# A list scheduler's model of a shared port, and new due steps, in a fused attention and gated-MLP kernel

## The chip, the cores and the metric

The kernel runs on one core of one Trainium2 chip. The metric is the device time of one execution in microseconds (us); the median of three executions is given. PE is the matmul engine (TensorE), DVE VectorE, ACT ScalarE, POOL GpSimd, SP SyncE, whose queue issues nearly all DMAs here. PSUM is the memory that matmuls write, SBUF the one that they read.

## The reference

Cut to what is computed:

```python
B, H, S, Ns, D = (8, 8, 512, 32, 64)          # x: B H S D, state: B H Ns D
scores = scale * np.matmul(x, state.transpose(0, 1, 3, 2))
a = softmax(scores)                            # over Ns
xread = np.matmul(a, state)
scores2 = scale * np.matmul(state, x.transpose(0, 1, 3, 2))
a2 = softmax(scores2)                          # over S
sread = np.matmul(a2, x)
attn = np.concatenate([xread, sread], axis=2)
x2 = attn.transpose(0, 2, 1, 3).reshape(B * (S + Ns), H * D)    # 4352 x 512
h = x2 @ w_in                                  # w_in: 512 x 2048
g = h * np.cos(h)
return (g @ w_out).astype(np.float32)          # w_out: 2048 x 512
```

`x` and `state` are float32; `w_in` and `w_out` come as float64, so the kernel turns their bits into float32 itself.

## The kernel before

For each of the eight batches the kernel does the attention, then makes `h` in tiles of 128 of the 2048 columns by the 512 tokens: 16 tiles a batch. `products` multiplies the states into `w_in`, so that a tile needs only the attention weights `aT` and those products `sw` (L488). Batches go in pairs. For the first pair a tile is 512 columns wide and has one of two PSUM banks; later tiles are done two at a time and partly with seven instead of eight block products (`seven_part`, L543). Each tile then goes through four gate steps: ACT makes a whole number of turns of `h` (`gate`, L564), DVE takes the difference (`gate2`, L567), ACT takes a sine (`gate3`, L570), DVE multiplies with `h` into `g_all` (`gate4`, L584). `gate4` is the last reader of the bank, so tile n + 2 can start on PE when `gate4` of tile n is done. Tiles are numbered from 0; the first pair has 32.

The second product, `g @ w_out`, has two forms. The first pair's batch 0 multiplies directly (`first_product` and `second_product`, L640). All others use sums of blocks (`Product`), whose matmuls are L772 and whose sums of `g_all` are L715 (POOL, some DVE). The block sums of `w_out` are made by `inner_weight` (L689) and `sums_of` (L1325), sent to DRAM (L677, L692) and fetched back into a ring (L706).

Eighteen conversions turn float64 pieces of `w_in` and `w_out` into float32. Each is a DMA of the raw bits (`fetch`, L210), two ACT steps (L223, L226), two DVE steps ("b" L229, "c" L232) and a POOL step ("d", L237). Raw pieces share buffers, so a later fetch waits for the L232 of the piece before it in the buffer.

The order of the first pair's work is not written out by hand. `first_pair_tasks` lists tasks with an engine, an assumed cost, what they read and write, and a due step; `link` derives the dependencies and turns due steps into due times; `first_pair` then goes through model time and picks for each engine the task that comes next, and issues it. A task with `shares` set is one of DVE that uses the SBUF port that DVE and POOL share. `CONV` and `CONV_DUE` give the order of the conversions and their due steps, `PACE` the model time of one step, `NEAR` how far apart starts may lie to be chosen between. The engines run what they get in order; the waits on the chip follow from the data alone, and the model's times are nowhere in the program. From step 32 on, `later_pair` and fixed plans (`plan`, `plan_products`) set the order.

The choice in the model, word for word:

```python
                soon = min(starts.values())
                t = min((t for t in mine if starts[t] <= soon + NEAR),
                        key=lambda t: t.due + 1.0 * (starts[t] - soon))
                if best is None or starts[t] < best[0]:
                    best = starts[t], t
```

The softmax of a batch's first scores goes through `shift` (L348), `exp1` (L352), `sums1` (L325), an inverse (L373, L374), `spread1` (L332) and `norm1` (L393); that of the second through `max2` (L343), `exp2` (L361), `turn` (L400), `turn_kept` (L405), `reads` (L417), `keep_scaled` (L436). `tokens` (L271) and `tokens_kept` (L280) turn a batch's tokens, which L1180 loads.

Of the kernel before, what the change touches and what calls it, by code (L numbers as in the profile page):

```python
# [22 lines left out]
def kernel(  # L23
# [46 lines left out]
    TEMPS = 4  # L70
# [5 lines left out]
    def matrix(n):  # L76
        return quad(n).rearrange("p t (u d) -> p (t u) d", d=HD)
# [972 lines left out]
    for n in range(B // 2):  # L1050
        end = n == B // 2 - 1
# [71 lines left out]
    def first_pair_tasks():  # L1123
# [49 lines left out]
        def attention(b, k):  # L1173
# [26 lines left out]
            for j in range(2 if b == 0 else 0):  # L1200
                add("act", act(512) + .03,
                    lambda j=j: a.exp1(slice(j, j + 1)), f"z{z}{j}",
                    f"z{z}{j}", k + 4)
            m2 = k + 6 if b == 0 else k + 5
            if b == 0:
                for j in range(2):
                    add("dve", .62, lambda j=j: a.sums1((j,)), f"z{z}{j}",
                        f"m1{j}", k + 5)
                add("dve", .46, a.inverse1, "m10 m11", "m10 m11", k + 5)
                for j in range(2):  # L1210
                    add("dve", .62, lambda j=j: a.spread1(slice(j, j + 1)),
                        f"m1{j}", f"xT{j}", k + 5)
                for j in range(2):
                    add("dve", .62, lambda j=j: a.norm1(slice(j, j + 1)),
                        f"z{z}{j} xT{j}", f"z{z}{j}", k + 5, True)
# [3 lines left out]
            if b == 0:  # L1219
                add("act", .2, a.exp2_bias, "m20 m21", "m20 m21", m2)  # L1220
                for j in range(2):
                    add("act", .72, lambda j=j: a.exp2((j,)),
                        f"at{j} m2{j}", f"xT{2 + j} i2{j} T", m2)
                add("dve", .3, a.inverse2, "i20 i21", "i20 i21", m2 + 2)
            else:
                add("act", 5.0, a.exps, "at0 at1 m20 m21",
                    f"z{z}0 z{z}1 xT2 xT3 i20 i21 m20 m21", m2)
                for j in range(2):
                    add("dve", .62, lambda j=j: a.sums1((j,)), f"z{z}{j}",
                        f"m1{j}", k + 6)  # L1230
                add("dve", .8, a.inverse12, "m10 m11 i20 i21",
                    "m10 m11 i20 i21", k + 7)
                for j in range(2):
# [215 lines left out]
        for step, what in (  # L1449
# [6 lines left out]
                                "sd00 sd01", "stT1", 6)),  # L1456
                (5, lambda: attention(1, 5.0)),
                (7, lambda: products(0, 2, 7)),
# [6 lines left out]
                (16, lambda: products(1, 1, 19)),  # L1465
                (16, lambda: inner(3, matrix(SQ), SQ, temps[1], E, 15)),
                (17, lambda: sums_of(A22, SQ, A11, sub_, 18, "pool")),
                (17, lambda: attention(2, 18)),
                (18, lambda: sums_of(A21, A11, A21, sub_, 19, "dve")),
                (20, lambda: products(1, 2, 23)),  # L1470
                (20, lambda: inner(5, matrix(A21), A21, temps[0],
                                   names(TEMPS), 20)),
                (20, lambda: sends(1, a12, 6, 22)),
# [4 lines left out]
                (24, lambda: products(1, 3, 27)),  # L1478
                (25, lambda: attention_late(2, 23.0)),
                (24, lambda: [add("sp", .4, lambda n=n: fetch_block(n), "B3",  # L1480
# [3 lines left out]
        for step, what in (  # L1484
                (26, lambda: outer(0, 2, 0, 0, 26, "dve")),
                (27, lambda: outer(0, 2, 0, 1, 27, "dve")),
                (28, lambda: tokens_of_next(30)),
                (28, lambda: products(2, 0, 28)),
                (28, lambda: p5_tasks(29.5)),
                (29, lambda: weight_columns(t32, 30)),  # L1490
                (29, lambda: add("dve", .7, lambda: halves(2, 0), "z00 z01",
                                 "E0", 30)),
                (29, lambda: add("dve", .7, lambda: halves(2, 1),
                                 "z00 z01 E0", "E1", 30)),
                (30, lambda: seven_tasks(t32, 30)),
                (31, lambda: weight_columns(t34, 32)),
                (32, lambda: outer(2, 3, 2, 0, 32, "dve")),
                (32, lambda: p3_sums(32))):
            at_step[step].append(what)
        for step, t in enumerate(all_tiles[0:FIRST]):  # L1500
            for what in at_step[step]:
                what()
            tile_(t, step)
            if 4 <= step < 4 + NH:
                first(step - 4, step + 1)
            for i in range(NH):
                if SECOND_AT[i] == step:
                    second(i, step + 2)
        for what in at_step[FIRST]:
# [4 lines left out]
    CONV = (4, 5, 6, 7, 8, 9, 10, 11, 14, 15, 16, 17, 12, 13)  # L1514
    CONV_DUE = (3, 4.5, 3.5, 6, 7.5, 7, 9, 9.5, 10.5, 11, 12, 14.5, 14, 15)
    PACE, NEAR, SEND = 3.8, 0.3, 2.5

# [36 lines left out]
    def first_pair():  # L1554
# [19 lines left out]
        lanes = 22.0  # L1574
        pool_busy, cold = (0.0, 0.0), True
        log = []
        while can:
            best = None
            for e in free:
# [4 lines left out]
                for t in mine:  # L1584
                    at_ = max(free[e], ready[t])
                    if t.shares and pool_busy[0] <= at_ < pool_busy[1]:
                        at_ = pool_busy[1]
                    starts[t] = at_
                soon = min(starts.values())
                t = min((t for t in mine if starts[t] <= soon + NEAR),  # L1590
                        key=lambda t: t.due + 1.0 * (starts[t] - soon))
                if best is None or starts[t] < best[0]:
# [13 lines left out]
            if t.engine == "pool":  # L1606
                pool_busy = at_, end
            if t.engine == "sp":
                size = {"x": .13, "Q": 1.05, "B": .26, "r": .26}.get(
# [137 lines left out]
```

## Time and profile before

| what | before |
|---|---|
| median of 3 executions | 740.53 us |
| lowest and highest | 739.6 and 740.9 us |
| profiled execution, its own time | 740.65 us |
| its span, from first to last instruction | 738.9 us |
| mean granted clock of PE | 0.993 |
| PE waiting for L584 in 20 to 165 us | 12.3 us, 9 times |
| L584 of tiles 2, 9, 16, 24, 31 ends at | 40.6, 73.8, 105.4, 140.4, 163.6 us |

The durations that follow come from the one profiled execution. Times inside it count from its first instruction. A busy PE in the profile is not a PE at its peak, since matmuls overlap; what counts for PE is its idle time and its clock.

### The profile page before, as it was taken

To read this page: it belongs to the slowest core of one execution; us is meant where nothing else is said; L and a number is where in the kernel's file an instruction comes from. 1 tells how busy PE (TensorE), PEld (TensorE's weight loads), DVE (VectorE), ACT (ScalarE), POOL (GpSimd) and SP (SyncE) were. 2 spreads that over 40 slices of the span, in tenths; PEclk is the share of its full clock that TensorE was granted. 3 is DMA by queue.
4 is the path that set the end of the run, shared out by engine and by line. 5 is a ranking of instruction groups with operands and counts; after the bars stand their busy time and mean duration, and the time that the engine had idled before them with its cause. 6 is when DMAs were issued, how large, how long until landed. Compare 5 with 4: busy or idle time off the path is not lost.

```text
span 738.9 us, 10734 instructions
## 1 busy us (share of the span) xinstructions
PE 708.2 (96%) x3626; PEld 519.0 (70%) x3626; DVE 506.8 (69%) x703; ACT 347.3 (47%) x586; POOL 542.5 (73%) x524
## 2 busy tenths in 40 slices
PE   8898889999999999999999999999999999999997
PEld 3343343477778878777778788777688788888886
DVE  4989979957866668849756577768665467355550
ACT  5799675654463446343634464344634533211110
POOL 1557789375998997588998665879989665799600
PEclk9999999999999999999999999999999999999999
DMA  9966799536346964693238635762225466456662
GB/s 297 285 192 193 236 265 301 122 96 150 87 128 117 214 172 115 142 197 86 82 80 168 160 96 116 147 154 83 75 68 119 115 205 143 108 156 203 155 152 46
DMA packets 204021, 111.33 MB, mean 151 GB/s; under 512 B 149888, under 2 KB 166784, under 8 KB 203968
## 3 DMA queue, kind: packets, MB, share of 16 engines
q1 hardware_dynamic: 202880, 110.14, 57.4%
q8 instruction: 29, 0.48, 0.3%
q10 hardware_dynamic: 960, 0.39, 0.2%
q14 instruction: 24, 0.20, 0.1%
q0 software_dynamic: 128, 0.13, 0.1%
HBM read 87.03 MB, written 23.59 MB: 150 GB/s over the span
## 4 chain that ended last, share of the span: by engine, by line
PE 59%; POOL 21%; DVE 9%; issue 3%; DMA 3%; ACT 2%; SPq 1%; ACTq 0%; POOLq 0%; DVEq 0%
PE o L772 29%; POOL g_all L715 16%; PE h L543 13%; PE h L488 8%; POOL swS_all L521 3%; PE at L312 3%; PE at L877 2%; DMA held<-in_state_dram 2%; PE o L640 2%; POOL sw_all L521 2%; DVE g_all L715 1%; PE at L417 1%; DVE q_all L567 1%; DVE g_all L232 1%; DVE g_all L584 1%
## 5 line engine op out<-in xcount | busy, mean ns | idle before, releaser
L715 POOL TENSOR_TENSOR g_all<-g_all 128x512 f32<-128x512 f32 x252 | 332.5, 1349 | 61.8 <-DVE g_all L715 40.4
L772 PE MATMUL o<-g_all 128*128 128x256 f32 x1456 | 343.7, 381 | 2.4 <-POOL g_all L715 2.4
L772 PEld LDWEIGHTS o<-g_all 128*128 128x128 f32 x1456 | 273.7, 190 | 49.7 <-issue 5.7
L567 DVE TENSOR_TENSOR q_all<-q_all,h 128x1024 f32<-128x1024 int32 (+1 forms) x88 | 85.3, 971 | 40.7 <-ACT q_all L564 40.4
L564 ACT ACTIVATE q_all<-h 128x1024 int32<-128x1024 f32 (+1 forms) x88 | 73.1, 833 | 81.2 <-PE h L543 35.1
L584 DVE TENSOR_TENSOR g_all<-h,q_all 128x1024 f32<-128x1024 f32 (+1 forms) x88 | 85.7, 973 | 24.5 <-ACT q_all L570 23.6
L570 ACT ACTIVATE q_all<-q_all,halfpi 128x1024 f32<-128x1024 f32 (+1 forms) x88 | 84.2, 957 | 38.7 <-DVE q_all L567 38.5
L551 DVE TENSOR_TENSOR h<-h,sums_all 128x256 f32<-128x256 f32 x96 | 41.3, 430 | 77.5 <-PE h L543 60.2
L488 PE MATMUL h<-aT_all,sw_all 128*128 128x512 f32 x128 | 64.0, 628 | 13.0 <-DVE g_all L584 12.3
L543 PE MATMUL h<-aT_all,sw_all 128*128 128x256 f32 x192 | 59.6, 392 | 3.8 <-DVE g_all L584 3.4
L543 PE MATMUL h<-aS_all,swS_all 128*128 128x256 f32 x192 | 60.2, 395 | 2.6 <-ACT sums_all L529 1.8
L715 DVE TENSOR_TENSOR g_all<-g_all 128x1024 f32<-128x1024 f32 x42 | 62.0, 1490 | 0.1
L543 PE MATMUL h<-aS_all,sw_all 128*128 128x256 f32 x192 | 58.0, 384 | 0.1
L488 PEld LDWEIGHTS h<-aT_all,sw_all 128*128 128x128 f32 x128 | 23.2, 195 | 44.3 <-issue 21.5
L521 POOL TENSOR_TENSOR swS_all<-sw_all 128x128 f32<-128x128 f32 x48 | 22.5, 468 | 41.8 <-ACT sw_all L462 41.8
L543 PEld LDWEIGHTS h<-aS_all,swS_all 128*128 128x128 f32 x192 | 33.9, 189 | 27.0 <-issue 12.1
L780 ACT COPY o<-o 128x256 f32<-128x256 f32 x26 | 9.3, 357 | 85.1 <-PE o L772 85.1
L543 PEld LDWEIGHTS h<-aT_all,sw_all 128*128 128x128 f32 x192 | 34.5, 189 | 16.3 <-DVE g_all L584 12.2
L237 POOL TENSOR_TENSOR w_in<-w_in,aS_all 128x1024 int32<-128x1024 int32 (+1 forms) x10 | 22.3, 2241 | 29.9 <-DVE w_in L232 27.2
L787 ACT COPY o<-sums_all 128x256 f32<-128x256 f32 x26 | 9.8, 378 | 68.2 <-PE o L772 68.2
L543 PEld LDWEIGHTS h<-aS_all,sw_all 128*128 128x128 f32 x192 | 35.6, 190 | 8.2 <-DVE h L551 2.7
L607 DVE SCALAR_TENSOR_TENSOR held<-o,held 128x512 f32<-128x512 f32 x38 | 25.9, 681 | 13.7 <-PE o L772 13.1
(116 smaller groups left out, 931.6 us busy)
## 6 DMA issues: line engine op xcount, KB each, us to landing
g_all<-blocks_kept SPq DMA_DIRECT2D x206, 256.0 KB, 2.8
blocks_kept<-g_all SPq DMA_DIRECT2D x48, 256.0 KB, 3.9
g_all<-in_moe_w_out_dram SPq DMA_DIRECT2D x8, 1024.0 KB, 5.7
out_dram<-ot SPq DMA_DIRECT2D x128, 64.0 KB, 2.0
g_all<-in_moe_w_in_dram SPq DMA_DIRECT2D x6, 1024.0 KB, 7.1
x_b<-in_x_dram SPq DMA_DIRECT2D x24, 256.0 KB, 4.7
xT<-in_x_dram SPq DMA_DIRECT2D x80, 64.0 KB, 2.8
x_b<-in_x_dram SPq DMA_DIRECT2D x16, 128.0 KB, 4.3
```

The lines of the kernel that those rows point to most:

```text
L237: nc.gpsimd.tensor_tensor(bits, bits, e, op=ALU.add)
L488: nc.tensor.matmul(out=t.hp, lhsT=t.lhs(i), rhs=t.rhs(i), start=(i == 0), stop=(i == t.kn - 1))
L521: nc.gpsimd.tensor_tensor(o, x1, x2, op=op)
L543: nc.tensor.matmul(out=out_, lhsT=w, rhs=r, start=start, stop=True, skip_group_check=True)
L551: nc.vector.tensor_tensor(o, h2[:, LO], sums_all[:, 0], op=ALU.add)
L564: nc.scalar.activation(t.q.bitcast(I32), t.hp, func=ACTF.Copy, bias=0.25)
L567: nc.vector.tensor_tensor(t.q, t.q.bitcast(I32), t.hp, op=ALU.subtract)
L570: nc.scalar.activation(t.q, t.q, func=ACTF.Sin, bias=halfpi, scale=-TWO_PI)
L584: nc.vector.tensor_tensor(g, t.hp, t.q, op=ALU.mult)
L607: nc.vector.scalar_tensor_tensor(out=out.t[:, ch], in0=bank, scalar=TWO_PI, in1=b.t[:, ch], op0=ALU.mult, op1=ALU.add)
L715: engine.tensor_tensor(o[:, i:i + n], x1[:, i:i + n], x2[:, i:i + n], op=ALU.subtract)
L772: nc.tensor.matmul(out=o, lhsT=ring[(self.first + k) % NB][:, i], rhs=g[:, i], start=(start and i == 0), stop=(i == QT - 1), skip_group_ch ...
```

## The change

Only the planner of the first pair is edited. In its model, a POOL task now waits while a DVE task that shares the port runs, as DVE's sharing tasks already did for POOL's; among tasks that can start nearly together, a later start weighs 8.0 instead of 1.0 against the due time. The small inverses and the halves are marked as sharing. Due steps of conversions, of two attention parts, of weight sums, of the direct products and of product p5 are set anew, and `PACE` goes from 3.8 to 4.0. The tasks themselves, what they compute and their assumed costs stay. Line numbers after the edit are those of before up to L1203; `sums_of` goes from L1325 to L1327.

```diff
-            m2 = k + 6 if b == 0 else k + 5
+            m2 = k + 6 if b == 0 else k + 4
...
-                add("dve", .46, a.inverse1, "m10 m11", "m10 m11", k + 5)
+                add("dve", .46, a.inverse1, "m10 m11", "m10 m11", k + 5,
+                    True)
...
-                add("dve", .3, a.inverse2, "i20 i21", "i20 i21", m2 + 2)
+                add("dve", .3, a.inverse2, "i20 i21", "i20 i21", m2 + 2,
+                    True)
...
                 add("dve", .8, a.inverse12, "m10 m11 i20 i21",
-                    "m10 m11 i20 i21", k + 7)
+                    "m10 m11 i20 i21", k + 7, True)
...
-                (5, lambda: attention(1, 5.0)),
+                (5, lambda: attention(1, 4)),
...
-                (16, lambda: inner(3, matrix(SQ), SQ, temps[1], E, 15)),
+                (16, lambda: inner(3, matrix(SQ), SQ, temps[1], E, 18.5)),
                 (17, lambda: sums_of(A22, SQ, A11, sub_, 18, "pool")),
-                (17, lambda: attention(2, 18)),
+                (17, lambda: attention(2, 19)),
...
                 (20, lambda: inner(5, matrix(A21), A21, temps[0],
-                                   names(TEMPS), 20)),
+                                   names(TEMPS), 20.5)),
...
-                (25, lambda: attention_late(2, 23.0)),
+                (25, lambda: attention_late(2, 27)),
...
-                (28, lambda: p5_tasks(29.5)),
+                (28, lambda: p5_tasks(30.5)),
...
                 (29, lambda: add("dve", .7, lambda: halves(2, 0), "z00 z01",
-                                 "E0", 30)),
+                                 "E0", 30, True)),
                 (29, lambda: add("dve", .7, lambda: halves(2, 1),
-                                 "z00 z01 E0", "E1", 30)),
+                                 "z00 z01 E0", "E1", 30, True)),
...
             if 4 <= step < 4 + NH:
-                first(step - 4, step + 1)
+                first(step - 4, step + 3)
             for i in range(NH):
                 if SECOND_AT[i] == step:
-                    second(i, step + 2)
+                    second(i, step + 2.5)
...
     CONV = (4, 5, 6, 7, 8, 9, 10, 11, 14, 15, 16, 17, 12, 13)
-    CONV_DUE = (3, 4.5, 3.5, 6, 7.5, 7, 9, 9.5, 10.5, 11, 12, 14.5, 14, 15)
-    PACE, NEAR, SEND = 3.8, 0.3, 2.5
+    CONV_DUE = (3, 1.5, 3.5, 6, 6, 7, 9, 9.5, 9.0, 11, 13.5, 12.3, 14, 15)
+    PACE, NEAR, SEND = 4.0, 0.3, 2.5
...
-        pool_busy, cold = (0.0, 0.0), True
+        pool_busy = dve_busy = 0.0, 0.0
+        cold = True
...
-                    if t.shares and pool_busy[0] <= at_ < pool_busy[1]:
-                        at_ = pool_busy[1]
+                    held_by = (pool_busy if t.shares else
+                               dve_busy if e == "pool" else (0.0, 0.0))
+                    if held_by[0] <= at_ < held_by[1]:
+                        at_ = held_by[1]
                     starts[t] = at_
...
-                        key=lambda t: t.due + 1.0 * (starts[t] - soon))
+                        key=lambda t: t.due + 8.0 * (starts[t] - soon))
...
             if t.engine == "pool":
                 pool_busy = at_, end
+            if t.shares:
+                dve_busy = at_, end
```

## The prediction

> **What bounds the kernel now.** I read the page first: its span, the engines' busy line, and the slices of the matmul engine.
>
> ```profile
> span 738.9 us, 10734 instructions
> PE 708.2 (96%) x3626; PEld 519.0 (70%) x3626; DVE 506.8 (69%) x703; ACT 347.3 (47%) x586; POOL 542.5 (73%) x524
> ...
> PE   8898889999999999999999999999999999999997
> ```
>
> PE is busy all the time but in the first slices of 18.5 us, about the first pair of batches. That is the part that the list scheduler writes; everything after it is ordered by other code. So the change is worth what it does to PE's idle time before about 164 us, provided that PE stays full afterwards. The waits from 20 to 165 us say whom PE waits for (in total, times, longest):
>
> ```profile
> PE h L488 <- DVE g_all L584: 12.3, 9, 3.5
> ```
>
> The windows between the gate ends of tiles 2, 9, 16, 24 and 31 say where (length, then busy PE, PEld, DVE, ACT, POOL, then clock, DMA share, GB/s):
>
> ```profile
> 40.60:73.80 33.20, 31.18 (x124) 13.30 (x124) 29.82 (x40) 31.65 (x45) 22.80 (x11) 1.00 0.61 183
> 73.80:105.40 31.60, 24.56 (x108) 10.25 (x109) 30.39 (x31) 22.07 (x38) 25.49 (x12) 0.89 0.86 249
> 105.40:140.40 35.00, 33.41 (x162) 15.04 (x160) 30.95 (x40) 22.05 (x41) 30.13 (x22) 1.00 0.76 236
> 140.40:163.60 23.20, 22.86 (x92) 13.94 (x91) 17.06 (x26) 12.93 (x26) 13.96 (x16) 1.00 0.45 101
> ```
>
> PE waits for L584, the DVE step that frees a tile's PSUM bank. The damage is in the second stretch: DVE 30.39 of 31.60, PE only 24.56, its clock down to 0.89. In the first stretch ACT is the fullest beside PE (31.65 of 33.20). The timelines of DVE, then of POOL, show why DVE is full (start, length):
>
> ```profile
> 79.19 1.21 DVE L232 SCALAR_TENSOR_TENSOR g_all<-g_all 128x1024 int32<-128x1024 int32 x1
> ...
> 83.19 3.40 DVE L232 SCALAR_TENSOR_TENSOR g_all<-g_all 128x1024 int32<-128x1024 int32 x1
> ```
>
> ```profile
> 83.17 2.34 POOL L237 TENSOR_TENSOR g_all<-g_all,aS_all 128x1024 int32<-128x1024 int32 x1
> ```
>
> The same instruction takes 1.21 us, or 3.40 when a Pool instruction began 0.02 us before it.
>
> **What the skill says.** The Trainium skill, SBUF — State Buffer, section "Who interferes with whom": DVE and GpSimd share a port pair as an exclusive lock; a DVE instruction with two SBUF inputs (against a Pool operation that reads SBUF) or in a two-port mode waits until the other is done. The trace agrees: 83.17 + 2.34 = 85.51, and from there to the next DVE start, 86.52, is 1.0, about its price alone. The small `tensor_scalar` of L373, which the change now marks as sharing, took 0.55 us at 126.82 and 2.03 at 70.84. Going through DVE's timeline, I find time over the free price of 3.9 us in the first stretch, 8.0 in the second, 4.9 and 1.8 after. TensorE: Matmul & The Clock Gate, Part 1, says that an idle array is clocked down: tile 11's four matmuls take 2.90 us after an idle 2.02, against 1.88 otherwise.
>
> **The change, part by part.** No instruction and no semaphore wait is added or removed in kind: the waits of Pool for DVE stand in the planner's model, and the dues, the weight 8.0 in the choice and the new marks act only through the order it writes. What counts is what each engine's order holds between the marks. I price it with the free duration, from a start to the next start: 0.60 for L567, L584, a reduce, a spread (L332) or L393; 0.62 + 1.14 for a conversion on DVE (L229, L232); 1.28 and 1.13 for a wide sum (L1325, L715); ACT 0.48 a gate, 0.63 a sine, 1.05 a conversion step; PE 1.72 a tile or a product pair (L640), 1.02 for attention or L312 groups. Work between gate ends, before and after, in us:
>
> | tiles | profiled | PE | ACT | DVE |
> |---|---|---|---|---|
> | 2 to 9 | 33.2 | 26.0, 29.4 | 29.6, 27.0 | 25.4, 27.7 |
> | 9 to 16 | 31.6 | 23.2, 19.7 | 22.6, 22.0 | 22.1, 16.6 |
> | 16 to 24 | 35.0 | 32.6, 29.9 | 19.0, 18.2 | 25.6, 24.7 |
> | 24 to 31 | 23.2 | 22.8, 22.1 | 12.3, 13.7 | 14.9, 15.4 |
>
> The second row is the change. DVE loses one conversion (1.76) and two spreads of batch 1 (1.2) to the first stretch and two sums L1325 (2.56) to the third: 5.5. PE loses two products (3.44) to the first. In the third, both L393 of batch 2 (1.2) and two L715 (2.3) leave DVE; reads (1.02) and a product (1.72) leave PE. At tile 31 PE has 3.5 less done than before (124.8 against 128.3); that stays to be paid.
>
> *Start to tile 2.* The inverse of 1.25 + 0.08 on DVE no longer stands ahead of tile 0's L584, so PE may reach tile 2 some 1.3 earlier; but ACT has 2.6 more ahead of tile 2's sine. I take no change: 40.6.
> *Tiles 2 to 9.* ACT was 3.6 short of filling 33.2; the fullest is now PE: 29.4 + 3.6 = 33.0, or 31.1 with PE's own loss there (27.7 for 26.0). DVE with the old blocking gives 27.7 + 3.9 = 31.6. I take 32.5: tile 9 at 73.1, little gain but with more done.
> *Tiles 9 to 16.* DVE before: 22.1 + 8.0 = 30.1, 1.5 short of 31.6. After: 10 sharing operations for 14; at the old 0.57 each, 16.6 + 5.7 + 1.5 = 23.8. So even without fewer collisions DVE stops being the bound. Late next is ACT: 22.0 + 3.6 = 25.6. I take 25.5: tile 16 at 98.6, for 105.4.
> *Tiles 16 to 31.* PE is fullest; old shortfalls 2.4 and 0.4 give 32.3 and 22.5: 153.4, for 163.6.
> *Sum.* 10.2 earlier, less 3.5 of PE work still to do: **6.7**. The profiled execution took 740.65 (738.9 is its span); 740.65 − 6.7 = 733.95, and the median stands 0.12 under it: **733.8**.
>
> *Taken at nothing.* SP: a second weight fetch (L210) now stands ahead of batch 1's eight loads (L1180, from 29.34, 7.3 to issue). It waits for the L232 of conversion 5, which moves from 32.3 to near 28, so the loads start about as before; a delay of up to 4 us is covered, as the first transpose ran at 39.3 and the last load is used at 45.4. Batch 2's four loads stand together, ahead of block sends they stood among: no loss. POOL: the same operations; the four L689 after the early conversions are split round one, and two L715 move ahead of three L689 (the other two stay behind). From its last conversion (106.1) to the first product sums (134.1) took 28; starting from about 95 it ends near 123, and PE's second L772 group, which reads them, comes near 142. If that cover were gone PE would wait us for us. After tile 31, PE's waits up to 215 us are 0.42 each, and what starts there waits for PE, so a lead is kept.
>
> **Rivals.**
> 1. *The collisions come with the new order.* The model holds Pool back, the chip does not; other pairs may meet. For: Pool is busy 25.5 of 31.6. Against: 14 sharing operations become 10 where it counts. First stretch 27.7 + 4.5 + 3.9 = 36.1, second 16.6 + 5.7 + 3.6 = 25.9, then 32.3 and 22.5: tile 31 at 157.4, 6.2 less 3.5: 2.7 gained, **737.9**.
> 2. *Better than summed.* PE bounds also the first two stretches, with 31.1 and 19.7 + 2.4, and tile 2 gains its 1.3: 11.5 + 1.3 = 12.8, **727.8**.
> 3. *Slower: a late fetch on ACT.* Each raw buffer is refilled after its L232, and ACT's L223 on it stands in order ahead of gates. By my times the chain of one buffer (conversions 14, 17, 13) leaves some 4 us beyond the 5.7 from issue to landing. The DMA share was 0.86 there, and 27 us of transfers must now fit 25.5. From a landing over about 10 us on, each generation delays all gates: at 13, three times 3 = 9 lost, 6.7 gained: **743**. Against: ACT waited only some 3 us in all for these fetches before.
> 4. *It does nothing*: the lead is eaten at the handover by Pool or by loads, **740.5**. Against: Pool waited there for ACT (7.8 us) and for a load, both behind PE.
>
> **How the numbers follow.** The summed case has 0.48, rival 2 0.12, rival 1 0.17, rival 4 0.07, rival 3 0.16. A measurement can tell about 0.2% (1.5 us) from no change: 0.76 faster (some of rival 1 goes to the same), 0.08 the same, 0.16 slower. The range runs from 726.0, a little beyond rival 2, to 741.0, which takes in rivals 1 and 4; most of rival 3 is left out.
>
> **What would show it.** Right: tile 16's L584 near 98.6 and tile 31's near 153; in the waits before 160, PE behind L584 falls from 12.3 to under 6; L229 and L232 on `g_all` at means near 0.9 and 1.3 (now 1.29 and 1.63); PE's clock near 1.0 between 73 and 98. Wrong: tile 9 later than 76; ACT waiting over 5 us for weight fetches; or tile 31 early and the end not.

## The result, and the profile after

The change makes the kernel slower: **746.15 us** (median of 5 executions, 743.21 to 747.14) against 740.49 (739.2 to 740.9), a ratio of 1.0078 with the 95% interval [1.0064, 1.0091]. The forecast was 733.8. The profiled execution of after took 744.28 us, 3.6 more than that of before (0.4 of it outside the span); the two single executions show less of the loss than the medians do (5.7). All the traces below are single executions too, and the one of before has some 1.2 us in its start that do not come from its order: three kernels with an unchanged start of before (run_in_before, before_late, before_moves, below) end tile 2 at 39.3 to 39.7, where the profile of before has 40.6. The granted clock of PE (1.00 is full speed) differs there: from 9 to 11.5 us it is 0.50 in the profile of before and 1.00 in before_late, and over the first 20 us 0.91 in before and 1.00 in all three.

The page of after:

```profile
span 742.1 us, 10735 instructions
...
PE 709.5 (96%) x3626; PEld 518.9 (70%) x3626; DVE 509.5 (69%) x703; ACT 347.0 (47%) x586; POOL 544.9 (73%) x524
...
PE   8888699999999999999999999999999999999997
```

The engines are as busy as before, and the loss is again in the first slices. The fifth slice (74 to 93 us) has the lowest digit: 6, where it was 8.

The waits of after, 20 to 165 us (in total, times, longest):

```profile
ACT q_all L570 <- DVE q_all L567: 20.6, 16, 4.7
...
PE h L488 <- DVE g_all L584: 11.6, 7, 6.2
```

PE waits for L584 almost as long as before (12.3), but in fewer, longer pieces: the longest was 3.5 us and is 6.2.

The windows between the gate ends of tiles 2, 9, 16, 24 and 31, with the stretch ahead of them (length, busy PE, PEld, DVE, ACT, POOL, clock, DMA share, GB/s):

```profile
0.00:44.10 44.10, 35.82 (x181) 16.29 (x182) 31.47 (x51) 28.60 (x44) 16.79 (x17) 0.96 0.91 274
44.10:78.30 34.20, 31.44 (x121) 12.75 (x121) 33.23 (x43) 29.78 (x42) 23.54 (x12) 0.95 0.58 190
78.30:107.70 29.40, 21.76 (x103) 8.98 (x102) 24.32 (x25) 21.87 (x39) 20.96 (x12) 0.88 0.80 216
107.70:140.30 32.60, 32.12 (x130) 14.02 (x130) 29.34 (x37) 19.63 (x33) 30.17 (x20) 1.00 0.84 267
140.30:163.30 23.00, 22.37 (x109) 12.70 (x108) 16.99 (x27) 15.01 (x32) 14.21 (x15) 1.00 0.53 104
```

| stretch | before | forecast | after |
|---|---|---|---|
| start to tile 2 | 40.6 | 40.6 | 44.1 |
| 2 to 9 | 33.2 | 32.5 | 34.2 |
| 9 to 16 | 31.6 | 25.5 | 29.4 |
| 16 to 24 | 35.0 | 32.3 | 32.6 |
| 24 to 31 | 23.2 | 22.5 | 23.0 |

Tile 31 ends at 163.3, as before (163.6). The 3.5 us of PE work that the new order leaves for later then come on top: the first L772 of after ends 4.5 us later than before, and from 170 us to the end PE's groups are 3.2 or 3.3 later.

What keeps the stretch 9 to 16 from its forecast, the timelines of after show. DVE (start, length) from 78 us on:

```profile
78.21 1.95 DVE L229 TENSOR_SCALAR g_all<-g_all 128x1024 int32<-128x1024 int32 x1
80.20 2.19 DVE L232 SCALAR_TENSOR_TENSOR g_all<-g_all 128x1024 int32<-128x1024 int32 x1
82.31 4.50 DVE L393 TENSOR_TENSOR aT_all<-aT_all,xT 128x512 f32<-128x512 f32 x2
86.73 1.27 DVE L567 TENSOR_TENSOR q_all<-q_all,h 128x512 f32<-128x512 int32 x2
```

POOL beside it:

```profile
77.24 2.37 POOL L237 TENSOR_TENSOR g_all<-g_all,aS_all 128x1024 int32<-128x1024 int32 x1 [2.75 <-DVE g_all L232]
79.69 3.82 POOL L1327 TENSOR_TENSOR g_all<-g_all 128x512 f32<-128x512 f32 x2
83.48 2.78 POOL L237 TENSOR_TENSOR g_all<-g_all,aS_all 128x1024 int32<-128x1024 int32 x1
```

And PE:

```profile
88.94 3.78 PE L488 MATMUL h<-aT_all,sw_all 128*128 128x512 f32 x4 [6.24 <-DVE g_all L584]
```

Four DVE steps that share the port stand in one run ahead of the L567 of tiles 10 and 11, the two tiles that then hold both PSUM banks. Their free price is 0.62 + 1.14 + 2 × 0.6 = 3.0 us; they take 8.5 (78.21 to 86.73), since POOL goes from one operation to the next beside them and each DVE step waits for one of POOL's. PE stands still for 6.24 us, and its next tile, clocked down, takes 3.78 instead of 1.9. The window around it, with the columns of the windows above, has the clock at 0.50:

```profile
86.00:92.00 6.00, 3.06 (x4) 1.18 (x4) 5.12 (x7) 3.26 (x6) 1.37 (x2) 0.50 0.59 168
```

In before no more than three stood between two gate steps in this stretch. Somewhat earlier before, too, has four in a row, ahead of the L567 of tile 8. DVE, then PE, of before:

```profile
60.18 1.74 DVE L229 TENSOR_SCALAR w_in<-w_in 128x1024 int32<-128x1024 int32 x2
61.84 2.39 DVE L232 SCALAR_TENSOR_TENSOR w_in<-g_all,w_in 128x1024 int32<-128x1024 int32 x2
```

```profile
63.76 5.31 PE L640 MATMUL o<-g_all 128*128 128x512 f32 x12
```

That row takes 3.9 us for a free price of 3.5, since POOL stands idle for 2.44 us of it, and PE does not wait, since it has three products to do. So more than its length makes the row of after costly: it has POOL's operations beside it, and PE has nothing else to do.

At the start, the L567 of tile 2 in before:

```profile
37.48 0.69 DVE L567 TENSOR_TENSOR q_all<-q_all,h 128x512 f32<-128x512 int32 x1 [1.50 <-ACT q_all L564]
```

The start of after, DVE:

```profile
36.48 1.96 DVE L373 TENSOR_SCALAR i_all<-i_all 128x2 f32<-128x2 f32 x1
...
40.69 1.22 DVE L232 SCALAR_TENSOR_TENSOR g_all<-g_all 128x1024 int32<-128x1024 int32 x1
41.94 1.29 DVE L567 TENSOR_TENSOR q_all<-q_all,h 128x512 f32<-128x512 int32 x2
```

And ACT:

```profile
22.84 1.12 ACT L223 ACTIVATE g_all<-g_all 128x1024 f32<-128x1024 f32 x1 [2.17 <-DMA g_all<-in_moe_w_out_dram]
23.85 0.64 ACT L462 COPY sw_all<-h 128x256 f32<-128x256 f32 x2
```

The L567 of tile 2, whose turns ACT had made by 37.4, stands behind the second inverse, the L427 and conversion 6, and starts at 41.94. And ACT waits 2.17 us for the raw bits of conversion 6, with the copies L462 that PE's tile 0 needs queued behind.

### The profile page after: what moved, and what is told of

Read it like the earlier page. It is cut to its first block, busy times and chain, and to the rows that moved or that the text cites. A ratio compares the mean times of both kernels' runs of the same rounds, so it can differ in the third digit from the quotient of the medians.

```text
span 742.1 us, 10735 instructions
## 1 busy us (share of the span) xinstructions
PE 709.5 (96%) x3626; PEld 518.9 (70%) x3626; DVE 509.5 (69%) x703; ACT 347.0 (47%) x586; POOL 544.9 (73%) x524
## 4 chain that ended last, share of the span: by engine, by line
PE 57%; POOL 21%; DVE 11%; ACT 4%; issue 4%; DMA 1%; SPq 1%; DVEq 0%; POOLq 0%
PE o L772 29%; POOL g_all L715 16%; PE h L543 13%; PE h L488 7%; POOL swS_all L521 3%; PE at L312 3%; PE at L877 2%; PE at L417 2%; POOL sw_all L521 2%; ACT q_all L570 1%; DVE g_all L584 1%; DVE g_all L715 1%; PE o L877 1%; DMA blocks_kept<-g_all 1%; DVE i_all L325 1%
## 5 line engine op out<-in xcount | busy, mean ns | idle before, releaser
L772 PE MATMUL o<-g_all 128*128 128x256 f32 x1456 | 343.9, 381 | 2.4 <-POOL g_all L715 2.4
L772 PEld LDWEIGHTS o<-g_all 128*128 128x128 f32 x1456 | 274.0, 190 | 48.8 <-issue 5.2
L567 DVE TENSOR_TENSOR q_all<-q_all,h 128x1024 f32<-128x1024 int32 (+1 forms) x88 | 85.2, 970 | 44.3 <-ACT q_all L564 44.1
L564 ACT ACTIVATE q_all<-h 128x1024 int32<-128x1024 f32 (+1 forms) x88 | 73.2, 833 | 82.1 <-PE h L543 38.1
L570 ACT ACTIVATE q_all<-q_all,halfpi 128x1024 f32<-128x1024 f32 (+1 forms) x88 | 83.9, 956 | 45.8 <-DVE q_all L567 45.6
L584 DVE TENSOR_TENSOR g_all<-h,q_all 128x1024 f32<-128x1024 f32 (+1 forms) x88 | 85.6, 974 | 22.6 <-ACT q_all L570 21.6
L488 PE MATMUL h<-aT_all,sw_all 128*128 128x512 f32 x128 | 65.3, 640 | 14.6 <-DVE g_all L584 11.6
L488 PEld LDWEIGHTS h<-aT_all,sw_all 128*128 128x128 f32 x128 | 23.5, 197 | 46.9 <-issue 20.9
L543 PEld LDWEIGHTS h<-aT_all,sw_all 128*128 128x128 f32 x192 | 34.5, 190 | 16.3 <-DVE g_all L584 12.1
L237 POOL TENSOR_TENSOR w_in<-w_in,aS_all 128x1024 int32<-128x1024 int32 (+1 forms) x10 | 22.0, 2215 | 28.7 <-DVE w_in L232 24.5
L607 DVE SCALAR_TENSOR_TENSOR held<-o,held 128x512 f32<-128x512 f32 x38 | 25.9, 680 | 13.7 <-PE o L772 13.1
```

The costliest lines, as they stand in the source:

```text
L488: nc.tensor.matmul(out=t.hp, lhsT=t.lhs(i), rhs=t.rhs(i), start=(i == 0), stop=(i == t.kn - 1))
L543: nc.tensor.matmul(out=out_, lhsT=w, rhs=r, start=start, stop=True, skip_group_check=True)
L564: nc.scalar.activation(t.q.bitcast(I32), t.hp, func=ACTF.Copy, bias=0.25)
L567: nc.vector.tensor_tensor(t.q, t.q.bitcast(I32), t.hp, op=ALU.subtract)
L570: nc.scalar.activation(t.q, t.q, func=ACTF.Sin, bias=halfpi, scale=-TWO_PI)
L584: nc.vector.tensor_tensor(g, t.hp, t.q, op=ALU.mult)
```

## The experiments

**How they are made.** In the kernels with moves the plan is made as in the kernel that they start from; then single steps are put ahead of another one in the order of their engine, and nothing else is changed. `gate_n`, `gate2_n`, `gate3_n` and `gate4_n` are the four steps of tile n (L564, L567, L570, L584), `conv16c` is the third step of conversion 16, `norm1_0` and `norm1_1` are the two L393 of batch 1. The other kernels differ in lines of the planner. Each was timed in 5 rounds beside the kernel before; medians of before were 739.4 to 739.6.

| kernel | starts from | median us | ratio to before [95%] |
|---|---|---|---|
| gates_first | after | 741.57 | 1.0036 [1.0023, 1.0049] |
| pool_swap | after | 742.71 | 1.0051 [1.0036, 1.0066] |
| copy_first | after | 743.41 | 1.0068 [1.0047, 1.0089] |
| all_moves | after | 742.50 | 1.0044 [1.0031, 1.0057] |
| start_moves | after | 742.51 | 1.0036 [1.0022, 1.0049] |
| run_in_before | before | 743.12 | 1.0043 [1.0027, 1.0060] |
| before_late | before | 739.84 | 1.0009 [1.0001, 1.0018] |
| before_moves | before | 743.22 | 1.0053 [1.0040, 1.0067] |
| dues_only | before + new dues | 740.05 | 1.0005 [0.9995, 1.0015] |
| dues_moves | dues_only | 741.73 | 1.0028 [1.0016, 1.0039] |
| dues_w8 | dues_only + weight 8.0 | 742.72 | 1.0040 [1.0024, 1.0055] |
| dues_hold | dues_only + hold | 746.89 | 1.0093 [1.0079, 1.0108] |
| dues_hold_gates | dues_hold | 746.54 | 1.0089 [1.0075, 1.0102] |
| before_hold | before + hold | 745.73 | 1.0080 [1.0064, 1.0096] |
| model_only | before + hold, weight, marks | 744.56 | 1.0064 [1.0049, 1.0080] |
| hold_back | after without hold | 742.12 | 1.0033 [1.0020, 1.0046] |
| weight_back | after with weight 1.0 | 744.36 | 1.0075 [1.0054, 1.0095] |
| hold_list | after, hold mended | 746.01 | 1.0088 [1.0074, 1.0102] |

### The run on DVE: gates_first and pool_swap

```diff
# gates_first, on DVE
+ gate2_10 ahead of conv16c; gate2_11 ahead of norm1_0; gate4_10 ahead of norm1_1
# pool_swap, on POOL
+ conv16d (L237) ahead of the two L1327
```

> The changed kernel with DVE's gate steps of tiles 10 and 11 moved in between the four operations that share the port (L229, L232, L393, L393) instead of behind them. Theory of runs (four sharing operations in a row, each held up by Pool, put 8.5 us ahead of both tiles' gates, when both banks were waiting): L584 of tile 10 ends near 85.5 instead of 88.9, PE's longest wait falls from 6.2 to about 3, and the kernel takes some 3 us less, about 743. Theory of sums: the same work in the stretch, 746.

> The changed kernel with POOL's two sums (L1327) moved behind the last step of conversion 16 (L237), so that Pool idles while DVE's run of four sharing operations begins. If the port is what makes that run 8.5 us long: L232 near 1.2 instead of 2.2 and the run near 6, some 2 us less, 744. If the run's length alone matters, or Pool is late for what follows: no change or slower, 746 to 748.

With the gate steps inside the run, L584 of tile 10 ends at 84.1 instead of 88.9, that of tile 12 at 90.8 instead of 95.6. Its trace was 0.6 ahead at tile 2 already, where nothing was moved. At tile 31 it is 3.3 us ahead of after, and the ratio falls from 1.0078 to 1.0036, 3.1 us. DVE, then PE, of gates_first:

```profile
80.03 1.70 DVE L232 SCALAR_TENSOR_TENSOR g_all<-g_all 128x1024 int32<-128x1024 int32 x1
82.21 0.69 DVE L567 TENSOR_TENSOR q_all<-q_all,h 128x512 f32<-128x512 int32 x1 [0.47 <-ACT q_all L564]
...
84.01 2.24 DVE L393 TENSOR_TENSOR aT_all<-aT_all,xT 128x512 f32<-128x512 f32 x1
```

```profile
84.15 3.10 PE L488 MATMUL h<-aT_all,sw_all 128*128 128x512 f32 x4 [2.05 <-DVE g_all L584]
```

PE waits 2.05 us there instead of 6.24. In pool_swap the order of DVE is that of after; only POOL's neighbours differ. DVE of pool_swap:

```profile
78.40 1.95 DVE L229 TENSOR_SCALAR g_all<-g_all 128x1024 int32<-128x1024 int32 x1
80.39 1.23 DVE L232 SCALAR_TENSOR_TENSOR g_all<-g_all 128x1024 int32<-128x1024 int32 x1
81.53 3.43 DVE L393 TENSOR_TENSOR aT_all<-aT_all,xT 128x512 f32<-128x512 f32 x2
```

The same run takes 6.5 us (78.40 to 84.89) instead of 8.5: its length depends on what POOL does beside it. The ratio falls to 1.0051, by 2.0 us. So the place of this run costs after some 3 us, and 2 of them come back when POOL's order alone is changed.

### A run made in before: run_in_before

```diff
# on DVE of the kernel before
+ conv17c, norm1_0 and norm1_1 ahead of gate2_12
```

> The kernel before with a run made in it: on DVE the L232 of conversion 17 and both L393 of batch 1 stand ahead of the difference of tile 12, where they stood one by one between the gate steps of tiles 12 and 13. Nothing is added. Theory of runs: L584 of tile 12 ends some 2.5 us later (near 90.3), that of tile 13 near 91 instead of 90.6, PE stands still for both banks at once, and the time is 1 to 2.5 us longer. Theory of sums: DVE has the same work between tiles 9 and 16, so tile 16 stays at 105.4 and the time within 0.5 us of before.

Nothing is added, and the kernel is 0.43% slower, 3.2 us. DVE and PE of run_in_before:

```profile
81.41 1.69 DVE L232 SCALAR_TENSOR_TENSOR g_all<-g_all 128x1024 int32<-128x1024 int32 x1
83.02 5.58 DVE L393 TENSOR_TENSOR aT_all<-aT_all,xT 128x512 f32<-128x512 f32 x2
```

```profile
90.74 3.78 PE L488 MATMUL h<-aT_all,sw_all 128*128 128x512 f32 x4 [4.56 <-DVE g_all L584]
```

Three steps of 2.3 us free price take 7.1; two L393 alone 5.58 for 1.2. PE waits 4.56 us and takes twice the time for the next tile. Tile 12 ends at 90.7, tile 13 at 92.8 (90.3 and 91 expected), though this trace was 1.1 us ahead of that of before at tile 2. The theory of sums, on which the forecast rested, allows none of this. The loss was larger than expected, since tile 13 was late as well.

### The start, and all moves together: copy_first, all_moves, start_moves

```diff
# copy_first, on ACT
+ the two copies L462 ahead of the L223 of conversion 6
# all_moves: copy_first, gates_first, and on DVE
+ gate4_7 ahead of conv11c
# start_moves: copy_first, gates_first, and on DVE
+ gate4_0 ahead of conv4b; gate2_1 ahead of conv4c; gate2_2 ahead of L373
+ gate4_2 ahead of conv6b; gate2_3 ahead of conv6c
# and on ACT
+ gate3_2 ahead of an L226
```

> The changed kernel with one move on ACT: the two copies of the first states' products (L462) stand ahead of the first step of conversion 6 (L223) again, as before the change. Theory of single stalls: tile 0 waited because ACT stood in order at a weight piece that had not landed (2.2 us); tile 1 ends on PE near 28 instead of 30.5, and the kernel takes some 2.5 us less than the changed one, about 743.6. Theory of sums (the order matters only by how much work each engine has in a stretch): nothing changes, 746.

> The changed kernel with the moves of ACT's copies and of the gate steps of tiles 10 and 11, and with the last gate step of tile 7 put ahead of the L232 that stood before it. Theory of runs and single stalls: 2.5 + 3 + 2.5 = 8 us less than the changed kernel, about 738, faster than before the change by some 2. Theory of sums: 746. If what one stall gives back is taken by the next: 742 to 744.

> The kernel after with the gates' steps moved ahead of the runs at tiles 10 and 11, as in gates_first, and at the start as well: on DVE the product of tile 0, the difference of tile 1, that of tile 2 and what follows them ahead of the conversion and the inverse, on ACT the copies L462 ahead of the weight step L223 and the sine of tile 2 ahead of L226. Theory of single stalls: tile 2 some 3 us earlier than in gates_first (near 40.5), tile 12 near 88, and the time near 738.5, a little below before. Theory that the next wait takes what a move gives: tile 2 earlier, but tile 12 at 90 to 91 and the time 741 to 742, as in gates_first.

copy_first brings tile 0 on PE from 27.9 to 23.9, but its L584 still ends at 34.6 (34.5 in after): conversion 4's L232 now meets a POOL L237 and takes 3.3 us instead of 1.2. Tile 2 ends 1.2 earlier, tile 12 1.0, tile 16 no earlier; all_moves, which contains the same move, ends tile 2 at 44.1, as after does, so that even the 1.2 may be a matter of the single execution. By the traces the wait of ACT at the start is thus no cause of the loss by itself. The times leave it open: the median of 743.41 is what the theory of single stalls expected (743.6), but its six executions run from 742.73 to 748.20, and the interval of its ratio takes in the 1.0078 of after. all_moves has tile 7 at 68.0 instead of 70.9, but tile 8 at 74.6 as after has it, and is no faster than gates_first. start_moves ends tile 2 at 39.4, 4.1 us earlier than gates_first, but tile 3 at 46.1 (45.9): two L229 ahead of its product take 3.44 us for 1.4, and on PE transposes L271 stand ahead of tile 4. Tile 12 ends at 91.1, and the time is that of gates_first. So what the start loses was not had back by these moves of gate steps; the next wait took it, as the second theory says.

### Which part of the edit: model_only, dues_only, hold_back, weight_back

```diff
# model_only: before with the edits of the model; dues_only: after with these taken back
-                    if t.shares and pool_busy[0] <= at_ < pool_busy[1]:
-                        at_ = pool_busy[1]
+                    held_by = (pool_busy if t.shares else
+                               dve_busy if e == "pool" else (0.0, 0.0))
+                    if held_by[0] <= at_ < held_by[1]:
+                        at_ = held_by[1]
...
-                        key=lambda t: t.due + 1.0 * (starts[t] - soon))
+                        key=lambda t: t.due + 8.0 * (starts[t] - soon))
# hold_back: after with the first of these taken back; weight_back: with the second
```

> The kernel before with the planner's model edits alone (POOL waits for DVE, weight 8.0, the new marks); due steps and PACE stay. Its DVE order starts as that of after does (the inverse L373 and four L427 and a conversion ahead of the difference of tile 2), and has L229 L232 L229 L232 L325 L325 ahead of the difference of tile 9. Theory of single stalls: the loss at the start comes from the model edits, so L584 of tile 2 ends near 44 and the time is 742 to 744. Theory that the new due steps do it: tile 2 near 40.6 and the time about 739.5, as before.

> The kernel after with the old model in its planner (DVE alone waits, weight 1.0, no new marks); the new due steps and PACE stay. Its DVE order has no conversion ahead of the difference of tile 2 and no run of four sharing steps ahead of tile 10. Theory of single stalls: tile 2 at 40.5 to 42, the time 739 to 741, about as before. Theory that the new due steps do it: tile 2 near 44 and 744 to 746, as after.

> The kernel after with one thing taken back in the planner's model: POOL no longer waits for DVE; weight 8.0, marks and due steps stay. Its DVE order has no conversion ahead of the difference of tile 2, and between tiles 9 and 11 one run ahead of the difference of tile 10 alone. Theory that the modelled hold writes the harmful order: tile 2 at 40 to 42 and the time 740 to 742. Theory that the weight 8.0 does: as after, tile 2 near 44 and 744 to 746.

> The kernel after with the weight of a later start at 1.0 again; the modelled hold, the marks and the due steps stay. Its DVE order begins as that of after, with the inverse and a conversion ahead of the difference of tile 2, and has L229 L232 L393 L393 ahead of the product of tile 10. Theory that the modelled hold writes the harmful order: tile 2 near 44 and the time 743 to 746. Theory that the weight 8.0 does: tile 2 near 40.6 and 739 to 741.

The new due steps alone cost nothing; in the trace of dues_only tile 2 ends at 40.6 and tile 31 at 160.5, and PE's waits for L584 are 5.1 us in all. The model edits alone cost 0.64%, with tile 2 at 42.5. Taking the hold back out of after gives more than half of the loss back (tile 2 at 39.8); taking the weight out gives nothing (tile 2 at 43.5). So the slower start needs the modelled hold of POOL. On the new due steps it needs the new marks too: dues_hold, in the next part, has the hold without them and ends tile 2 at 41.0. The marks alone were not run.

### The parts one by one: dues_hold, dues_w8, before_hold, dues_hold_gates

```diff
# dues_hold, before_hold: the hold alone, added to dues_only and to before
# dues_w8: the weight 8.0 alone, added to dues_only
# dues_hold_gates: dues_hold, and on DVE
+ gate2_10 ahead of conv16c; gate2_11 ahead of norm1_0; gate4_10 ahead of norm1_1
```

> The kernel dues_only with the modelled hold of POOL added, and nothing else. Its DVE order has the run L229 L232 L393 L393 ahead of the differences of tiles 10 and 11, as after has it, but nothing ahead of the difference of tile 2. Theory of runs: tile 2 at 40 to 42, L584 of tile 12 at 91 to 94 (dues_only: 86.4), and the time 741.5 to 743.5. Theory of sums: tile 12 near 86.4 and the time near 740.

> The kernel dues_only with the weight of a later start at 8.0, and nothing else. Its order has no run that stands ahead of two tiles' gates but L229 L232 L393 ahead of the difference of tile 11, which dues_only has too. Theory that the hold alone does the harm: 739.5 to 741, as dues_only. Theory that the weight takes part: over 742.

> The kernel before with the modelled hold of POOL added, and nothing else. Its DVE order has runs of four to six steps ahead of the products of tiles 7 and 9 (L229 L229 L232 L232; L229 L232 L229 L232 behind an inverse) and of the product of tile 10. Theory of runs: L584 of tile 12 at 91 or later (before: 87.8) and the time 742 to 745. Theory that the hold is harmless without the new due steps: 739 to 741.

> The kernel dues_hold with the three gate steps of tiles 10 and 11 moved ahead of their run, as in gates_first. Theory of runs: L584 of tile 12 some 4 us earlier than in dues_hold and the time 2 to 4 us shorter, 738 to 740. Theory that the next wait takes it: the time within 1 us of dues_hold.

The hold alone costs 0.9% on the new due steps and 0.8% on the old ones. dues_hold loses as much as after without the slower start (tile 2 at 41.0), so that the start is not what the loss hangs on. The weight alone costs 0.4% on the new ones, so the theory that the hold alone does the harm fails there; beside the hold it adds nothing (weight_back), and it may be what is left of the loss in hold_back (0.33%). In before_hold PE waits 5.22 us ahead of tile 11, behind a product that stood behind two conversions and the inverse. dues_hold has the run of after (78.72 to 87.24, 8.5 us, two L393 in 4.51), and tile 12 ends at 99.0. But dues_hold_gates is not faster by anything that the ratios can tell (1.0089 and 1.0093). There PE's order has L417 ahead of tile 12, L417 waits for ACT's copy L405, and L405 may write `xT` only when L393 has read it. PE, then ACT, of dues_hold_gates:

```profile
85.90 1.70 PE L417 MATMUL at<-x_b,xT 128*64 128x128 f32 x16 [3.04 <-ACT xT L405]
```

```profile
85.27 0.59 ACT L405 COPY xT<-at 128x512 f32<-128x512 f32 x1 [0.70 <-DVE aT_all L393]
```

The end of the run itself is waited for here, not only the gate steps behind it. Putting gates first moves the L393 back, and the wait changes its name.

### Does the hold hold? hold_list

```diff
-                    if held_by[0] <= at_ < held_by[1]:
-                        at_ = held_by[1]
+                    for b0, b1 in (pool_busy if t.shares else
+                                   dve_busy if e == "pool" else ()):
+                        if b0 <= at_ < b1 and at_ < 110:
+                            at_ = b1
...
-                dve_busy = at_, end
+                dve_busy.append((at_, end))
```

`dve_busy` in after is the last interval only. Once DVE's next sharing step is placed, a POOL step that could start earlier finds nothing to wait for. By the planner's own times the run above goes from 72.54 to 75.69, 3.2 us, with a POOL L1327 from 72.54 and an L237 from 75.04 right beside it: the plan overlaps what the chip takes in turn. Over the first pair the plan of after overlaps 21.4 us of marked DVE steps with POOL, that of before 18.7, that of dues_only 13.5 and that of hold_list 12.2. These do not follow the times: hold_list has the least and is among the slowest.

> The kernel after with the hold in the model made to remember every interval up to model time 110 instead of the last one, so that in the plan no sharing DVE step and no POOL step overlap there. The plan has L584 of tile 16 end at 100.2; in the plan of after it is 93.8, and the chip ended it at 107.7, 13.9 later (before: 96.0 in the plan, 105.4 on the chip, 9.4 later). Theory that the plan of after forgets the collisions: the chip comes at most 9 later than the plan, tile 16 at 105 to 109. Theory that other things than the port set the difference: it stays near 14 and tile 16 comes near 114. The order still has long runs ahead of tiles 7, 9 and 11, so the time is not expected to be better than before: 740 to 745.

Tile 16 ends at 106.8, 6.6 after its plan instead of 13.9 after: in this stretch the plan of after did forget the collisions. The kernel is not faster for it; with the collisions counted, the list still puts two conversions and more ahead of the products of tiles 7 and 9.

### Moves elsewhere: dues_moves, before_late, before_moves

```diff
# dues_moves, on DVE of dues_only
+ gate4_9 ahead of L332; gate2_11 ahead of conv16c; gate4_11 ahead of norm1_1
# and on ACT
+ gate_10 ahead of an L223; gate_11 ahead of an L226; L405 and gate3_11 ahead of an L226
# before_late, on ACT and DVE of before
+ gate_14 ahead of L223, gate3_14 ahead of L436; gate2_14 ahead of conv12b; gate4_14 ahead of conv12c
# before_moves: before_late, and on DVE
+ gate4_8 ahead of L373; gate4_9 ahead of conv16b; gate4_10 ahead of conv17b
```

> The kernel dues_only with seven steps between tiles 9 and 13 moved forward on their engine: on DVE the product of tile 9 ahead of L332, the difference of tile 11 ahead of an L232, its product ahead of an L393; on ACT the turns of tile 10 ahead of an L223, those of tile 11 ahead of an L226, the copy L405 and the sine of tile 11 ahead of another L226. Theory of single stalls: tile 11 and 13 on PE some 2 us earlier, tile 16 near 105 instead of 107.2, and the time 738 to 739, at or a little below before. Theory that the next wait takes it: tile 13 earlier, tile 24 as in dues_only (133.5), and 740.

> The kernel before with four steps of tile 14 moved forward on their engine and nothing else: on ACT its turns ahead of the L223 of conversion 12 and its sine ahead of L436; on DVE its difference ahead of the L229 and its product ahead of the L232 of that conversion. By the trace of before its product then ends near 94.1 instead of 97.2, so that PE waits some 0.5 instead of 3.48 before tile 16 and makes that tile at 1.9 instead of 3.68. Theory of single stalls: tile 16 on PE ends 3 to 4 us earlier (97 to 98 instead of 101.0), and 2 to 4 us of it are left at the end: 736 to 738. Theory that the next wait takes it: tile 16 earlier, tile 24 at 139 to 140.4 as before, the time 739 to 740.

> The kernel before with the four steps of before_late moved and three more on DVE: the product of tile 8 ahead of the inverse L373, that of tile 9 ahead of an L229, that of tile 10 ahead of an L229. Each stood 0.9 to 1.8 us behind such a step with its sine done. Theory of single stalls: tile 12 on PE ends 1 to 2 us earlier than in before (80.7), and the time is 1 to 2 us below that of before_late. Theory that the next wait takes it: the time of before_late within 0.7 us.

before_late does what was expected to tile 16, which PE ends at 95.8 instead of 101.0, and gains nothing (1.0009). PE of before_late:

```profile
93.78 1.98 PE L488 MATMUL h<-aT_all,sw_all 128*128 128x512 f32 x4 [1.28 <-DVE g_all L584]
97.39 1.98 PE L640 MATMUL o<-g_all 128*128 128x512 f32 x4 [1.63 <-POOL g_all L237]
...
102.96 1.98 PE L488 MATMUL h<-aT_all,sw_all 128*128 128x512 f32 x4 [1.75 <-DVE g_all L584]
```

The product L640 now waits for POOL's L237 of conversion 12, and tile 17 for the product of tile 15, which stands behind an L1325, an L229 and an L232 that end as late as before. Taking away PE's longest wait in before was worth nothing, because the chains through POOL and through DVE to the next tile were as long. dues_moves is of the same kind and lost 0.2% (tile 16 at 109.7, 107.2 in dues_only, 1.1 of it from its start); PE's longest wait is there for POOL's L237, 2.9 us.

before_moves did not test what its expectation says. The L584 that stood behind L373 in the trace of before is that of tile 9, not 8, and so on: the three moves put the products of tiles 8, 9 and 10 behind other steps instead of ahead of them (their ends at 70.6, 76.5 and 83.4, in before_late 66.6, 72.5 and 77.3). It shows that such products put 4 to 6 us back cost 2.9 us at tile 31. Whether the moves that were meant would gain anything was not tried.

No kernel was faster than before.

## Why the prediction was wrong, step by step

**Which step failed.** The sum per stretch. It took the work of the fullest engine, plus what it lost before, as the time of a stretch, and priced the blocking of each sharing operation alike (0.57 us), wherever it stood. The end of tile 31 came 9.9 us later than forecast, in these terms: start 3.5, tiles 2 to 9 1.7, tiles 9 to 16 3.9, the other two 0.3 and 0.5. The median came 12.3 above its forecast. Of the difference 0.4 lie outside the span, and 2.0 are what the medians differ by more than the two profiled executions; 1.2 of these are the slow start of the profile of before, and the rest stays open.

- *Tiles 9 to 16* (25.5, was 29.4). "Even without fewer collisions DVE stops being the bound" was right of its sum: it was busy 24.3 of 29.4. With 16.6 of free work that is 7.7 of blocking on ten sharing operations, for the 5.7 assumed. What set the end was the place of the collisions: one run with both banks behind it, 6.24 us of PE, and the tile after it at twice its time. The run costs some 3 us by gates_first; where the other 0.9 of this stretch went was not tested.
- *Start to tile 2* (no change, was 3.5 more). The prediction weighed 1.3 us less on DVE against 2.6 more on ACT. It didn't follow where the inverse went: ahead of the difference of tile 2, with a conversion, where it was blocked for 1.96 us. The hold and the marks together write that order (tile 2 at 39.8 without the hold in hold_back, 41.0 without the marks in dues_hold, 43.5 with both in weight_back).
- *Tiles 2 to 9* (32.5, was 34.2). DVE was full, 33.23 of 34.20, with 27.7 of free work: 5.5 of blocking for the 3.9 assumed. Conversions 14 and 11 stand in a row ahead of tile 7's product. The sign "tile 9 later than 76" came: 78.3. The reading that PE takes over two products here does not hold by the clock: in this stretch PE began 32 matmuls of L640 in before and 29 in after, in the next 8 and 7.
- *Fewer collisions.* Forecast means were 0.9 and 1.3 for L229 and L232 on `g_all`; they are 0.85 and 1.58. The groups of after, 20 to 165 us (busy, mean ns):

```profile
L232 DVE SCALAR_TENSOR_TENSOR g_all<-g_all 128x1024 int32<-128x1024 int32 x8 | 12.7, 1583 | 0.3
L232 DVE SCALAR_TENSOR_TENSOR w_in<-g_all,w_in 128x1024 int32<-128x1024 int32 (+1 forms) x8 | 10.5, 1327 | 0.1
L229 DVE TENSOR_SCALAR w_in<-w_in 128x1024 int32<-128x1024 int32 (+1 forms) x8 | 7.2, 926 | 0.0
L393 DVE TENSOR_TENSOR aT_all<-aT_all,xT 128x512 f32<-128x512 f32 x6 | 7.0, 1210 | 0.0
L229 DVE TENSOR_SCALAR g_all<-g_all 128x1024 int32<-128x1024 int32 x8 | 6.8, 850 | 0.7 <-ACT g_all L223 0.7
```

The five groups sum to 44.2 us; in before they were 13.0, 8.5, 5.1, 6.0 and 10.3, 42.9. L229 on `g_all` fell from 10.3 to 6.8, and the two groups on `w_in` and L393 took it up. The collisions moved and did not go, as rival 1 said; its price for tiles 9 to 16 was too low (25.9, measured 29.4), since it too spread them over a stretch.

**What held.** The 3.5 us of PE work left at tile 31; the two late stretches; the lead or lag kept unchanged to the end (3.2 us); nothing at the handover from SP or POOL. Rival 3's time (743) is the nearest, by chance: its mechanism, ACT behind a late fetch, shows only in 2.17 us at the start, not in the stretch that the rival named, and in the trace of copy_first nothing of that wait is left at tile 16.

**The port and the clock.** The Trainium skill, SBUF — State Buffer, section "Who interferes with whom", tells of an exclusive lock between DVE and GpSimd, and the traces agree; the prediction used it to price one collision and not a row of them, where each DVE step waits for another POOL step: 8.5 us for 3.0. TensorE: Matmul & The Clock Gate, Part 1, on which the prediction drew, puts the idling that halves the clock at about one window of 3.4 us. The halving is there (0.50 from 86 to 92 us in after), but a shorter idling was at times enough: 2.02 us ahead of tile 11 in before, 1.44 in dues_only.

**Why the hold does harm** is in part argued from the code. In the model of before a DVE step that would meet POOL starts late, so that a gate step can be chosen ahead of it; with the hold it is POOL that is put back in the model, the sharing steps are free to follow each other, and the list makes rows of them. On the chip POOL doesn't keep back. That the hold alone makes the kernel 0.8 to 0.9% slower on either set of due steps is shown; that it does so through rows of sharing steps is shown for the run at tile 10 in after; before_hold and dues_hold have such rows too, but in dues_hold the moves gave nothing back and in before_hold none was tried, and the other stretches were not tested. The plan itself was no guide: it had tile 31 of after 3.5 us earlier than that of before and that of dues_only 3.3 later; the chip ended them 0.3 and 3.1 earlier.

## What to carry to other kernels

Work that is summed over a stretch bounds its time from below; what an order costs shows in what stands ahead of the step that frees a buffer. Before trusting a new order, look in it for rows of instructions that share a port with another engine ahead of the releases of all buffers at once, and price such a row as its own work plus the other engine's work beside it. A single long wait that is taken away is worth only its distance to the next chain: the same three moves paid some 3 us in gates_first and nothing in dues_hold_gates, where the end of the row itself was waited for, and before_late gained nothing either.

## What the hardware showed beyond that

A row of blocked DVE steps alternates with POOL's operations, and both pay: two L393 of 1.2 us took 3.43 (pool_swap), 4.50 (after) and 5.58 (run_in_before), and in the row of after POOL's two half sums L1327 took 3.82 us for 2.5 without company (2.49 in dues_only, at 88.34).

PE's clock does not follow the length of the wait ahead of it alone. Over the traces of all these kernels, a tile of the first pair (four L488) took 1.95 to 1.99 us after each of 111 waits of up to 1.41 us, and 2.54 to 3.78 after each of 20 waits of 2.75 us or more (3.78 after the 6.24 in after). Between these lie 42 waits, and 18 of the tiles behind them were slow: 3.78 after 1.44 (dues_only, at 83.86, with another wait of 1.47 just before) and 3.10 after 2.05 (gates_first), but 1.99 after 2.07 (before, at 73.88) and 1.98 after 2.74 (pool_swap, at 71.11). So a wait of 1.4 us or more can cost up to 1.9 on top.
